# Two raw weights loaded before the attention's last stores, three half tiles made in the attention instead of four, and the sums of later pairs held back

## The chip, the cores and the metric

The kernel runs on one core of a Trainium2 chip. The metric is the device time of one launch in microseconds. Before the change it is 913.08 us, the median of three runs (912.22 to 913.17). The core has five engines with a queue each: PE (TensorE, the matmuls), ACT (ScalarE), DVE (VectorE), POOL (GpSimd) and SP, which here issues every DMA. Each engine takes its queue in order and waits where an operand isn't ready.

## The reference

Attention over 4 batches, 8 heads, 576 positions and 64 elements a head, causal with a window of 128 and a bias linear in the distance; then two feed-forward layers, each 512 -> 2048 -> 512, on 2304 tokens.

```
scores = where(0 <= rel < 128, q @ k.T / 8 - slope[h] * |rel|, -1e9)
x = softmax(scores) @ v                     # to (2304, 512)
h = x @ moe_w_in;   x = (h * cos(h)) @ moe_w_out
h = x @ moe2_w_in;  g = where(h >= 1, h, where(h <= -1, 0, (h + 1)**2 / 4))
out = g @ moe2_w_out                        # (2304, 512)
```

Inputs come as float32 for the attention, while the weights reach the kernel as 64-bit raw words.

## The kernel before, in words

Three of the kernel's habits matter. Every product of the feed-forward layers is made of three passes on TensorE with operands split into a high part (a ScalarE cast) and a low part (a subtraction, line 271). A raw weight of 512 KB is "decoded" to 32 bits by ScalarE and VectorE (lines 700 to 708, `decode`) and then split (lines 759 and 760). And tokens are worked in three chunks of 768: the first chunk of the first layer by plain products (`mm_a`, line 786, then `chain`, lines 795 to 811, then `mm_b`, line 825), the five others by a Strassen-like scheme that needs sums of weight blocks.

A half tile is one raw weight: number j is the input weight (j even) or output weight (j odd) of the column block f = j // 2, 32 in the first layer. The attention (`attention`, line 533) goes over 36 pairs in a pipeline; step k loads the operands of pairs k + 4 and k + 5, computes scores for pair k + 3, and stores x of pair k - 1 where x isn't kept on chip (line 518). SP's list is written in program order, so from step 13 on each step's loads stand behind the store of x of the step before. Beside this the attention "makes" the first half tiles: `halves` (line 325) is a generator that does one instruction group at each `make()`. `D_STEPS` (line 42) says at which steps `make()` is called; two more calls and a loop that empties the generator stand in the attention's tail (lines 609 to 616), ahead of the last copy and store of x. `stage_raw` (line 282) issues the load of a raw tile into one of three buffers, and after it any store of a made tile that is waiting.

After the attention everything of the two layers is put as operations into a planner (`Plan`). It takes TensorE's order as given, works out from costs (`COST`) when each operation is due, and simulates the engines from time 6.0 on; the order in which its simulated engines begin the operations is the order in which they are written to each queue. Where an operation has `after`, the simulation doesn't begin it earlier. None of these times is kept on the chip: there only the order and the data hold.

In the plan, `first_weights` loads, decodes and splits the half tiles that the attention didn't make. For every two column blocks, a pair p, `sum_steps` (line 310) makes the sums: four POOL steps (line 313), then twice a ScalarE cast (line 317), a POOL subtraction (line 271) and a store of 512 KB. For p < `EARLY` they follow at once on the decoded pair. For later pairs the decoded pair is stored to `ud` (line 768) and loaded again (`load_sum`, line 667) into one of two buffers `up`, which the input weights of the last four column blocks use too. The sums are needed by the second chunk (line 876 on). The second layer's weights are loaded from planned time 178 on.

Of the kernel before, what the change touches and what calls it, by code (L numbers as in the profile page):

```python
# [30 lines left out]
UNITS = (("A11", "A12"), ("S3", "S1"), ("S2", "S4"), ("A22",))  # L31


MADE = 4


AHEAD = 3
W2_FROM, W2_STEP = 178.0, 33.0
EARLY = 3


D_STEPS = (4, 9, 11, 13, 14, 15, 16, 18, 20)
PT = "DADADADD"
XE = "DA"
ORDERED = {ENG.DVE, ENG.Activation, ENG.Pool, ENG.SP}
# [187 lines left out]
def attention_moe_moe_kernel(  # L233
# [91 lines left out]
    def halves():  # L325

        def low_part(f, h):
            w = (win, wout)[h][f]
            u = (half_u(win_u[0], f), wout_u.get(f))[h]
            sub_lo(DVE, w[:, 1, :], u, w[:, 0, :])  # L330
            if not h:
                stores.append((lambda: move(fd[0][0][3], w[:, :, 256:512])) if f else (lambda: move(fd[0][0][0], w)))

        before = None
        for j in range(MADE):
            f, h = j // 2, j % 2
            stage_raw(0, j)
            if j + 1 < MADE:
                stage_raw(0, j + 1)
            t = raw64.pop((0, j))  # L340
            low, high = words(t)
            if h:
                wout_u[f] = u = two.tile([128, 512], F32, tag="wu", name=nm("wu"), bufs=U_BUFS)
            else:
                if f == 0:
                    win_u[0] = big("W", NF, "up", F32, (128, 4, 256))
                u = half_u(win_u[0], f)
            ui = u32(u)
            ACT.activation(u, high.bitcast(F32), AF.Copy, scale=2.0**-112)
            yield  # L350
            DVE.tensor_scalar(out=ui, in0=ui, scalar1=3, scalar2=0x7FFFFFFF,
                              op0=ALU.logical_shift_left, op1=ALU.bitwise_and)
            yield
            DVE.scalar_tensor_tensor(out=ui, in0=high, scalar=0x80000000, in1=ui,
                                     op0=ALU.bitwise_and, op1=ALU.bitwise_or)
            yield
            DVE.scalar_tensor_tensor(out=ui, in0=low, scalar=29, in1=ui,
                                     op0=ALU.logical_shift_right, op1=ALU.bitwise_or)
            if h:
                wout[f] = w = big("W", NF, "wo")  # L360
            else:
                win[f] = w = big("Q", Q_BUFS, "wi")
            ACT.copy(w[:, 0, :], u)
            if before:
                yield
                low_part(*before)
            before = f, h
        yield
        low_part(*before)
# [163 lines left out]
    def attention():  # L533
        for part in range(2):
            for n in range(3):
                load(n, (part,))
        make_identity(nc, ident)
        make_dist8()
        DVE.memset(half, 0.5)
        DVE.memset(half_pi, TWO_PI / 4)  # L540
        np_ = len(pairs)
        for k in range(-AHEAD, np_ - AHEAD - 1):
            new = pairs[k + AHEAD]
            mid = pairs[k + AHEAD - 1] if k + AHEAD >= 1 else None
            nrm = pairs[k + AHEAD - 2] if k >= 2 else None
            cur = pairs[k] if k >= 0 else None
            old = pairs[k - 1] if k >= 1 else None
            if k > -AHEAD:
                load(k + AHEAD + 1)
                load(k + AHEAD + 2)  # L550
            if k == 0:
                pe_t(cur)
            pe_s(new)
            if k > 0:
                pe_t(cur)
            if old:
                pe_v(old)
            scores(new, 0)
            if cur:
                copy_t(cur, 0)  # L560
            if nrm:
                normalise(nrm)
            if k >= 1:
                prepare(mid)
            scores(new, 1)

            if k in D_STEPS:
                make()
            while low_parts:
                low_parts.pop()()  # L570
            if mid:
                invert(mid, add=k < 1)
                if k < 1:

                    normalise(mid)
            if cur:
                copy_t(cur, 1)
            if old:
                put_x(old)

        p0, p1, p2, p3, p4 = pairs[np_ - 5:]
        pe_s(p4)
        pe_t(p1)
        pe_v(p0)
        scores(p4, 0)
        copy_t(p1, 0, "D")
        normalise(p2)
        invert(p3, add=True)
        normalise(p3)
        copy_t(p1, 1, "A")  # L590
        scores(p4, 1)
        pe_t(p2)
        pe_v(p1)
        copy_t(p2, 0, "D")

        ACT.activation(half_pi2, half, AF.Sin)
        put_x(p0, "A")
        invert(p4, add=True)
        normalise(p4)
        copy_t(p2, 1, "D")  # L600
        pe_t(p3)
        pe_v(p2)
        put_x(p1, "D")
        copy_t(p3, 0, "D")
        copy_t(p3, 1, "A")
        pe_t(p4)
        pe_v(p3)
        put_x(p2, "A")
        make()
        copy_t(p4, 0, "D")  # L610
        copy_t(p4, 1, "A")
        pe_v(p4)
        put_x(p3, "A")
        make()
        for _ in making:
            pass
        put_x(p4, "A")
        while stores:
            stores.pop(0)()
# [43 lines left out]
            gate = [part(kt, "T4", t4, k + 4)]  # L663
        return bt

    def load_sum(op, p, s, reads):
        op("S", "512", lambda: SP.dma_start(s.t, ud[p]), reads=reads, writes=[s])

    def moes():

# [10 lines left out]
            held.append(b)  # L681
            return b

        for f in range(2):
            wo[0][f] = ready("W", wout[f])
            wi[f] = ready("Q", win[f])
        pair0 = ready("W", win_u[0])
        g_res = [Res() for _ in range(NF)]
        for r in g_res:
            r.t = None  # L690
        kept = {tag: [b for b in held if b.tag == tag] for tag in ("W", "Q")}
        plan = Plan({"s": S_BUFS, "Q": Q_BUFS, "B": 14, "W": NF, "ld": LD_BUFS, "wu": U_BUFS, "so": SO_BUFS, "up": UP_BUFS},
                    {"s": [8.0] * 4, "ld": [9.0], "wu": [8.0], **kept})
        op = plan.op

        def s_buf(name, dtype=F32):
# [46 lines left out]
        def first_weights(j):  # L743
            f, h = j // 2, j % 2
            p = f // 2
            raw = Buf("ld", lambda: two.tile([128, 512], mybir.dt.int64, tag="ld", name=nm("wst"), bufs=LD_BUFS))
            op("S", "512", lambda: SP.dma_start(raw.t, w1[f, h]), writes=[raw])
            if h:
                u = Buf("wu", lambda: two.tile([128, 512], F32, tag="wu", name=nm("wu"), bufs=U_BUFS))
                ap = lambda: u.t  # L750
                wo[0][f] = w = Buf("W", lambda: big("W", NF, "wo"))
            else:
                if f % 2 == 0:
                    wi_u[p] = Buf("W", lambda: big("W", NF, "up", F32, (128, 4, 256))) if f < 12 else Buf("up", pair_tile)
                u = wi_u[p]
                ap = lambda: half_u(u.t, f)
                wi[f] = w = Buf("Q", lambda: big("Q", Q_BUFS, "wi"))
            decode(raw, u, ap)
            op("A", "hi512", lambda: ACT.copy(w.t[:, 0, :], ap()), reads=[u], writes=[w])
            op("D", "tt512", lambda: sub_lo(DVE, w.t[:, 1, :], ap(), w.t[:, 0, :]), reads=[u], writes=[w])  # L760
            if h:
                return
            if f % 2 == 0:
                op("S", "512", lambda: move(fd[0][p][0], w.t), reads=[w], writes=[fac[0][p][0]])
                return
            op("S", "256", lambda: move(fd[0][p][3], w.t[:, :, 256:512]), reads=[w], writes=[fac[0][p][3]])
            if p >= EARLY:
                op("S", "512", lambda: SP.dma_start(ud[p], u.t), reads=[u], writes=[ud_res[p]])
            else:
                sum_steps(op, 0, p, u, lambda: Buf("so", part_tile), lambda i: fac[0][p][i])  # L770
# [170 lines left out]

        sum_steps(op, 0, 0, pair0, lambda: Buf("so", part_tile), lambda i: fac[0][0][i])
        for f in range(NF):
            if 2 * f >= MADE:
                first_weights(2 * f)
                first_weights(2 * f + 1)
            mm_a(0, f)
            chain(0, f)
            if f:
                mm_b(0, f - 1)  # L950
            last = mm_a(1, f)
            chain(1, f)
            for g in (f - 2, f - 1) if f == 2 else (f - 1,) if f > 2 else ():
                mm_b(1, g)
            if f == 4:
                bt = prep(op, 0, 1, "DP", [last])
        for p in range(EARLY, NP):
            s = Buf("up", pair_tile)
            load_sum(op, p, s, [ud_res[p]])
            sum_steps(op, 0, p, s, lambda: Buf("so", part_tile), lambda i, p=p: fac[0][p][i])  # L960
        second_weights()
        fills = carry()
# [149 lines left out]
```

## Time and profile before

| | |
|---|---|
| median of three runs | 913.08 us |
| profiled execution: time, span | 916.26 us, 914.4 us |
| PE busy | 882.4 us (96%) |
| DVE, ACT, POOL busy | 668.9, 552.9, 264.2 us |
| granted PE clock, mean | 0.991 |
| DMA moved | 190.29 MB, 208 GB/s |

All times in the rows are microseconds from the start of the span. The attention's last matmul ends at about 127.5, the first chunk lasts to about 275, and the second chunk begins there. From 282 on PE hardly ever stands still. A row of a timeline may merge several like instructions (x12): its duration then reaches from the first to the last. In brackets stands the idle time of the engine before it and what ended it.

### The profile page before, as it was taken

What the parts mean: (1) busy time and instruction counts of PE and PEld (TensorE: products, weight loads), DVE (VectorE), ACT (ScalarE), POOL (GpSimd) and SP (SyncE); (2) the same over time, 40 slices, a digit from 0 to 9 for tenths busy, and PEclk for the clock granted to TensorE, in tenths of its full rate; (3) what the DMA queues carried; (4) which work ended last, traced back from release to release, by engine and by line L of the source; (5) the groups of instructions that cost most, each with busy time, mean ns of one, the idle gap of its engine ahead of it and who ended that gap; (6) DMA issues with size and microseconds to landing.
All of it is one profiled execution on the core that took longest, in us unless ns stands there. A gap on an engine that the chain in (4) does not pass through costs nothing. (4 is left out here: it accounts for less than half of the span.)

```text
span 914.4 us, 15792 instructions
## 1 busy us (share of the span) xinstructions
PE 882.4 (96%) x5472; PEld 832.2 (91%) x5472; DVE 668.9 (73%) x1404; ACT 552.9 (60%) x1257; POOL 264.2 (29%) x269
## 2 busy tenths in 40 slices
PE   7998987998999999999999999999999999999998
PEld 5776776877889999999999899999999999999998
DVE  6896869999875687997887897877555558355551
ACT  7886857877766577667777565655344445344440
POOL 5665654358332011671211750302200004000000
PEclk9998998999999999999999999999999999999999
DMA  8546736876887678658879578875154452444210
GB/s 300 176 136 209 213 119 207 298 260 229 267 298 249 207 250 311 242 211 318 277 285 328 196 264 312 271 277 182 49 196 161 162 168 75 138 161 162 93 35 34
DMA packets 81262, 190.29 MB, mean 208 GB/s; under 512 B 8224, under 2 KB 40992, under 8 KB 81184
## 3 DMA queue, kind: packets, MB, share of 16 engines
q1 hardware_dynamic: 81184, 189.30, 61.2%
q8 instruction: 43, 0.70, 0.3%
q14 instruction: 35, 0.29, 0.1%
HBM read 140.51 MB, written 48.76 MB: 207 GB/s over the span
## 5 line engine op out<-in xcount | busy, mean ns | idle before, releaser
L937 PE MATMUL y<-gh,wo 128*128 128x384 f32 x1280 | 339.5, 335 | 0.0
L876 PE MATMUL h<-b,wi 128*128 128x384 f32 x1680 | 305.5, 334 | 0.7 <-ACT c L884 0.6
L876 PEld LDWEIGHTS h<-b,wi 128*128 128x128 f32 x1680 | 292.2, 188 | 1.6 <-ACT c L884 0.9
L937 PEld LDWEIGHTS y<-gh,wo 128*128 128x128 f32 x1280 | 233.4, 188 | 0.0
L937 PE MATMUL y<-gl,wo 128*128 128x384 f32 x640 | 215.1, 336 | 2.8 <-DVE gl L271 2.7
L937 PEld LDWEIGHTS y<-gl,wo 128*128 128x128 f32 x640 | 120.7, 189 | 4.9 <-DVE gl L271 4.9
L313 POOL TENSOR_TENSOR up<-up 128x256 f32<-128x256 f32 x64 | 62.2, 972 | 212.2 <-DVE so L271 170.2
L884 ACT COPY c<-h 128x384 f32<-128x384 f32 x120 | 57.3, 478 | 94.5 <-PE h L876 90.4
L888 DVE TENSOR_TENSOR c<-h,c 128x384 f32<-128x384 f32 x120 | 66.4, 553 | 50.0 <-PE h L876 26.3
L914 ACT ACTIVATE t<-t,half 128x384 f32<-128x384 f32 x96 | 59.0, 618 | 59.1 <-DVE t L911 59.1
L451 ACT ACTIVATE sc<-sc,st 128x256 f32<-128x256 f32 (+1 forms) x144 | 70.1, 489 | 25.7 <-DVE st L444 22.3
L271 DVE TENSOR_TENSOR gl<-t,gh 128x384 fp32r<-128x384 f32 (+1 forms) x96 | 59.7, 622 | 33.5 <-ACT gh L894 29.9
L457 POOL TENSOR_TENSOR sc<-sc,st 128x512 f32<-128x512 f32 (+1 forms) x72 | 70.0, 993 | 41.8 <-DVE st L531 30.5
L643 POOL TENSOR_TENSOR xs<-xs,xs 128x384 f32<-128x384 f32 x20 | 26.6, 1331 | 180.4 <-DVE b L271 123.8
L786 PE MATMUL h<-x,wi 128*128 128x512 f32 (+1 forms) x384 | 72.3, 339 | 4.5 <-DVE t L801 4.5
L786 PEld LDWEIGHTS h<-x,wi 128*128 128x128 f32 x384 | 59.9, 190 | 13.8 <-DVE t L801 5.8
L271 DVE TENSOR_TENSOR gl<-g,gh 128x384 fp32r<-128x384 f32 x80 | 59.3, 778 | 7.2 <-PE y L937 3.1
L444 DVE CUSTOM_DVE_ANT_0 sc<-pa,dist 128x256 f32<-128x256 f32 (+1 forms) x144 | 52.4, 402 | 11.6 <-PE pa L429 11.4
L924 DVE TENSOR_TENSOR g<-c,t 128x384 f32<-128x384 f32 x80 | 47.6, 597 | 18.1 <-ACT t L914 9.8
L705 DVE TENSOR_SCALAR wst<-wst 128x512 uint16<-128x512 uint16 x60 | 52.3, 871 | 10.9 <-ACT wst L702 10.4
L271 POOL TENSOR_TENSOR so<-up,so 128x512 fp32r<-128x512 f32 x32 | 46.2, 1455 | 45.0 <-ACT so L317 45.0
L894 ACT CAST gh<-t 128x384 fp32r<-128x384 f32 x80 | 41.1, 514 | 18.1 <-DVE t L917 17.2
(90 smaller groups left out, 1230.3 us busy)
## 6 DMA issues: line engine op xcount, KB each, us to landing
wi<-fd SPq DMA_DIRECT2D x120, 512.0 KB, 4.6
wst<-in_w SPq DMA_DIRECT2D x64, 512.0 KB, 4.7
fd<-so SPq DMA_DIRECT2D x40, 512.0 KB, 4.9
qk<-in_qkv SPq DMA_DIRECT2D x36, 320.0 KB, 3.8
wi<-fd SPq DMA_DIRECT2D x40, 256.0 KB, 3.3
xs<-xd SPq DMA_DIRECT2D x40, 192.0 KB, 4.6
v<-in_qkv SPq DMA_DIRECT2D x36, 192.0 KB, 3.8
out_t<-ys SPq DMA_DIRECT2D x24, 192.0 KB, 1.9
```

Of the source, the lines that this page charges most:

```text
L271: eng.tensor_tensor(out=out, in0=full, in1=f32(hi), op=ALU.subtract)
L313: op("P", "tt256", lambda i=i, x=x, y=y, alu=alu: POOL.tensor_tensor(out=s.t[:, i, :], in0=s.t[:, x, :], in1=s.t[:, y, :], op=alu), writes ...
L444: DVE.tensor_tensor_reduce(out=sc[:, h, 0:w], in0=b[h], in1=dist8[2 * hp + h][:, 256 - w:256], scale=-0.125, scalar=3.0e38, op0=ALU.add, o ...
L451: ACT.activation(sc[:, h, 0:w], sc[:, h, 0:w], AF.Exp, bias=st[:, c:c + 1], scale=-1.0, accum_out=st[:, 4 + c:5 + c])
L457: POOL.tensor_tensor(out=sc[:, :, 0:w], in0=sc[:, :, 0:w], in1=st[:, 8 + 2 * j:10 + 2 * j].unsqueeze(2).to_broadcast([128, 2, w]), op=ALU. ...
L705: op("D", "ts16", lambda: DVE.tensor_single_scalar(out=quarters(raw.t)[:, :, 1], in_=quarters(raw.t)[:, :, 3], scalar=0x8000, op=ALU.bitwi ...
L786: PE.matmul(h, lhsT=wi[f].t[:, k, s], rhs=x, start=(n == 0), stop=(n == 11))
L876: PE.matmul(cell.t, lhsT=unit.t[:, a, s], rhs=bs[kt].t[:, x, :], start=(start and i == 0), stop=(stop and i == 5), skip_group_check=True)
L884: op("A", "copy384", lambda: ACT.copy(s.t, cell.t), reads=[bank[tag]], writes=[s])
L888: op("D", "tt384", lambda: DVE.tensor_tensor(out=s.t, in0=cell.t, in1=s.t, op=ALU.add), reads=[bank[tag]], writes=[s])
L914: op("A", "f384", lambda: ACT.activation(t.t, t.t, AF.Square, bias=half, scale=0.5), writes=[t])
L937: PE.matmul(cell.t, lhsT=w[:, a, s], rhs=x.t, start=(first and i == 0 and k == 0), stop=(last and i == 1 and k == 2), skip_group_check=True)
```

## The change

`MADE` goes from 4 to 3, so the output weight of block 1 (half tile 3) is no longer made in the attention. Instead, when the third half tile is begun, the raw loads of half tiles 3 and 4 are both issued, and the plan finds them as held buffers (`staged`) and only decodes them. `D_STEPS` gets one more step, 3, and the tail has one `make()` in place of the emptying loop. `EARLY` goes from 3 to 2, so that pair 2's sums go through `ud` as well, and `load_sum` gets a time, 64 + 15.6 p, before which the planner doesn't begin it.

```
-MADE = 4
+MADE = 3
-EARLY = 3
+EARLY = 2
+SUM_FROM, SUM_STEP = 64.0, 15.6
-D_STEPS = (4, 9, 11, 13, 14, 15, 16, 18, 20)
+D_STEPS = (3, 4, 9, 11, 13, 14, 15, 16, 18, 20)
...
-            if j + 1 < MADE:
-                stage_raw(0, j + 1)
+            stage_raw(0, j + 1)
+            if j + 1 == MADE:
+                stage_raw(0, j + 2)
...
         put_x(p3, "A")
         make()
-        for _ in making:
-            pass
+        make()
         put_x(p4, "A")
...
+    def load_sum(op, p, s, reads, after):
+        op("S", "512", lambda: SP.dma_start(s.t, ud[p]), reads=reads, writes=[s], after=after)
...
+        staged = {j: ready("ld", t) for (_, j), t in raw64.items()}
...
-                    {"s": [8.0] * 4, "ld": [9.0], "wu": [8.0], **kept})
+                    {"s": [8.0] * 4, "wu": [8.0], **kept})
...
+            raw = staged.get(j)
+            if not raw:
+                raw = Buf("ld", lambda: two.tile([128, 512], mybir.dt.int64, tag="ld", name=nm("wst"), bufs=LD_BUFS))
+                op("S", "512", lambda: SP.dma_start(raw.t, w1[f, h]), writes=[raw])
...
-            load_sum(op, p, s, [ud_res[p]])
+            load_sum(op, p, s, [ud_res[p]], SUM_FROM + SUM_STEP * p)
```

## Rows read from the trace of the kernel before

**Rows 1.** PE's waits from 127 to 282: total us, times, longest.
```profile
PE y L825 <- ACT gh L810: 7.4, 1, 7.4
PE h L786 <- DVE t L801: 4.5, 5, 1.5
PE y L825 <- DVE g L271: 1.9, 2, 1.0
```

**Rows 2.** PE's timeline in the first chunk: start, us, instruction, [idle before].
```profile
127.47 7.20 PE L786 MATMUL h<-x,wi 128*128 128x512 f32 x36
142.09 0.79 PE L825 MATMUL y<-gh,wo 128*128 128x512 f32 x1 [7.43 <-ACT gh L810]
...
158.24 2.91 PE L786 MATMUL h<-x,wi 128*128 128x512 f32 x12
...
166.57 2.91 PE L786 MATMUL h<-x,wi 128*128 128x512 f32 x12
...
193.07 3.02 PE L786 MATMUL h<-x,wi 128*128 128x512 f32 x12 [1.32 <-DVE t L801]
...
241.55 3.06 PE L786 MATMUL h<-x,wi 128*128 128x512 f32 x12 [0.49 <-DVE t L801]
```

**Rows 3.** Busy time by engine from 142 to 147, granted clock, DMA.
```profile
142.00:147.00 5.00, 4.91 (x12) 3.65 (x13) 4.88 (x7) 4.12 (x10) 1.40 (x1) 0.58 0.46 184
```

**Rows 4.** ACT's timeline around the long wait.
```profile
130.69 0.36 ACT L514 COPY x<-pa 128x256 f32<-128x256 f32 x1
136.17 0.66 ACT L700 ACTIVATE up<-wst 128x512 f32<-128x512 f32 x1 [5.12 <-DMA wst<-in_w]
...
137.28 0.58 ACT L795 ACTIVATE k<-h 128x512 int32<-128x512 f32 x1
...
141.42 0.62 ACT L810 CAST gh<-t 128x512 fp32r<-128x512 f32 x1
```

**Rows 5.** DVE's timeline: the attention's tail, the first decode, a later low part.
```profile
128.25 0.43 DVE L351 TENSOR_SCALAR wu<-wu 128x512 uint32<-128x512 uint32 x1 [1.12 <-ACT wu L349]
...
130.81 0.69 DVE L271 TENSOR_TENSOR wo<-wu,wo 128x512 fp32r<-128x512 f32 x1
137.41 0.74 DVE L705 TENSOR_SCALAR wst<-wst 128x512 uint16<-128x512 uint16 x1 [5.90 <-ACT wst L702]
...
156.28 0.73 DVE L271 TENSOR_TENSOR wi<-up,wi 128x512 fp32r<-128x512 f32 x1
```

**Rows 6.** SP's timeline: DMA issues in the attention, at its end, and later.
```profile
68.95 0.43 SPq L286 DMA_DIRECT2D wst<-in_w  x1
...
72.46 0.47 SPq L415 DMA_DIRECT2D qk<-in_qkv  x1
...
115.50 15.90 SPq L518 DMA_DIRECT2D xd<-x  x7
...
132.16 7.10 SPq L747 DMA_DIRECT2D wst<-in_w  x4
...
246.74 1.76 SPq L667 DMA_DIRECT2D up<-ud  x1
```

**Rows 7.** PE's timeline in the attention, scores of three pairs.
```profile
79.47 2.08 PE L429 MATMUL pa<-qk 64*128 64x256 f32 x8 [3.46 <-DMA qk<-in_qkv]
...
85.07 1.14 PE L429 MATMUL pa<-qk 64*128 64x256 f32 x8
...
88.18 1.22 PE L429 MATMUL pa<-qk 64*128 64x256 f32 x8
```

**Rows 8.** Groups from 127 to 282: count, busy us, mean ns, idle before.
```profile
L313 POOL TENSOR_TENSOR up<-up 128x256 f32<-128x256 f32 x32 | 30.6, 957 | 40.2 <-DMA up<-ud 24.2 <-DVE wi L271 7.7 <-ACT wo L363 6.5
L271 POOL TENSOR_TENSOR so<-up,so 128x512 fp32r<-128x512 f32 x16 | 23.4, 1476 | 28.6 <-ACT so L317 28.6
L708 DVE SCALAR_TENSOR_TENSOR up<-up,wst 128x512 uint32<-128x512 uint32 x14 | 13.4, 957 | 0.1
L801 DVE TENSOR_TENSOR t<-h,t 128x512 f32<-128x512 f32 x16 | 11.0, 688 | 1.4 <-ACT t L800 1.4
```

More of the change, by code (lines that the diff above doesn't have):

```diff
@@ L664, in prep @@
         return bt
-    def load_sum(op, p, s, reads):
-        op("S", "512", lambda: SP.dma_start(s.t, ud[p]), reads=reads, writes=[s])
+    def load_sum(op, p, s, reads, after):
+        op("S", "512", lambda: SP.dma_start(s.t, ud[p]), reads=reads, writes=[s], after=after)
     def moes():
@@ L682, in ready @@
             return b
-        for f in range(2):
-            wo[0][f] = ready("W", wout[f])
-            wi[f] = ready("Q", win[f])
+        for f, t in wout.items():
+            wo[0][f] = ready("W", t)
+        for f, t in win.items():
+            wi[f] = ready("Q", t)
+        staged = {j: ready("ld", t) for (_, j), t in raw64.items()}
         pair0 = ready("W", win_u[0])
@@ L690, in moes @@
             r.t = None
-        kept = {tag: [b for b in held if b.tag == tag] for tag in ("W", "Q")}
+        kept = {tag: [b for b in held if b.tag == tag] for tag in ("W", "Q", "ld")}
         plan = Plan({"s": S_BUFS, "Q": Q_BUFS, "B": 14, "W": NF, "ld": LD_BUFS, "wu": U_BUFS, "so": SO_BUFS, "up": UP_BUFS},
-                    {"s": [8.0] * 4, "ld": [9.0], "wu": [8.0], **kept})
+                    {"s": [8.0] * 4, "wu": [8.0], **kept})
         op = plan.op
@@ L745, in first_weights @@
             p = f // 2
-            raw = Buf("ld", lambda: two.tile([128, 512], mybir.dt.int64, tag="ld", name=nm("wst"), bufs=LD_BUFS))
-            op("S", "512", lambda: SP.dma_start(raw.t, w1[f, h]), writes=[raw])
+            raw = staged.get(j)
+            if not raw:
+                raw = Buf("ld", lambda: two.tile([128, 512], mybir.dt.int64, tag="ld", name=nm("wst"), bufs=LD_BUFS))
+                op("S", "512", lambda: SP.dma_start(raw.t, w1[f, h]), writes=[raw])
             if h:
@@ L943, in moes @@
         for f in range(NF):
-            if 2 * f >= MADE:
-                first_weights(2 * f)
-                first_weights(2 * f + 1)
+            for j in (2 * f, 2 * f + 1):
+                if j >= MADE:
+                    first_weights(j)
             mm_a(0, f)
```

## The prediction

> **What bounds the kernel now.** I read three views in order: who the engines waited for, TensorE's timeline around its longest wait, and then the other queues over the same microseconds. TensorE is busy for 96% of the span, so a change pays only where TensorE stands still or runs at the lower clock. Between the attention and the second chunk it waits for three things: once, 7.4 us, for a ScalarE cast of gh; five times, 4.5 us in all, for VectorE's product h*t; and twice, 1.9 us, for VectorE's low part of g [rows 1]. Together that is 13.8 us.
>
> The long wait lies at the start of the first product. TensorE begins it at 127.47, issues 36 matmuls in 7.20 us and then stands from 134.67 to 142.09 [rows 2]. The reader should follow that cast backwards. It belongs to a chain of ScalarE and VectorE that starts with a ScalarE step k at 137.28; ScalarE did nothing from about 131.05 to 136.17 because the instruction ahead of k, the decode of a raw weight, waited 5.12 us for its DMA [rows 4]. VectorE was idle 5.90 us for the same reason [rows 5]. That DMA was issued only at 132.16: SP takes its list in order, and its last seven stores of x hold it from 115.50 to 131.40 [rows 6]. The last store needs a ScalarE copy at 130.69, which stands behind the making of the fourth half tile [rows 4]. So one late store delays a load, the load blocks ScalarE's queue, and the blocked queue delays TensorE.
>
> **The change, part by part.** *Raw weights.* Half tiles 3 and 4 are now in the buffer long before the end of attention. ScalarE is free after the last copy of x. Without the fourth half tile ahead of it that copy waits for TensorE alone, which ends the attention at 127.47 [rows 2], so it ends near 127.9. Four decode steps of some 0.55 us (136.17 to 137.28 holds two [rows 4]) end at 130.1. The first product's h is ready after 12 of the 36 matmuls; 12 such matmuls take 2.91 us [rows 2], hence 130.4. So k can start at 130.4. Before, from the start of k at 137.28 to TensorE's restart at 142.09 were 4.8 us with decode steps between them [rows 2, 4]; I keep that length and get 135.2, where TensorE is ready at 134.67. The hole shrinks from 7.43 to about 0.5: -6.9. At best it goes fully, -7.4. At worst the load that is still late (the third raw buffer, issued near 128.5 behind the last x store) stands before k in ScalarE's order; with the 4.0 us from issue to decode [rows 4, 6] k would start at 133.1 and TensorE at 137.9, a hole of 3.2, or -4.2. I expect the better case, since that tile shares its 32-bit buffer with half tile 4 and can't be decoded before it.
>
> *Clock.* After the hole the granted clock is 0.58 for 5 us, and 12 matmuls take 4.91 us there [rows 3] against 2.91 us at full speed [rows 2]: 2.0 us at the lower level, 1.2 GHz. With a hole of 0.5 I count it all as gain, -2.0. After the waits of 1.32 and 0.49 us the next 12 matmuls took 3.02 and 3.06 us [rows 2], nearly the full clock. The other end is 0.
>
> *The fourth half tile.* From the attention's tail go three VectorE steps and a low part, the first of them after a wait of 1.12 us; VectorE ends there at 131.5 [rows 5] and should end near 127. The planned part gets a decode instead: three ScalarE steps, and on VectorE two decode steps and a low part of some 0.7 us each (the step at 137.41 and the low part at 130.81 [rows 5]), 2.1 us. These fall into the 5.90 us that VectorE lost before; if that cover is gone they delay the chains by 2.1 us at most. The tile is needed for the second output product, which comes after some 7 us more of TensorE work. I count 0. The made tiles' steps shift by one place in the attention; TensorE hardly waits there outside the one place below.
>
> *Sums held back.* A pair's sums are four POOL steps of 957 ns and two of 1476 ns, 6.8 us; 32 of the first kind, so all eight lots, run between 127 and 282 [rows 8]. While POOL works VectorE's steps are stretched: the decode's last step averages 957 ns there, against 688 ns of h*t, which has the same shape [rows 8]. The seven waits of 6.4 us lie between 193 and 242 [rows 2]. Spread evenly, one lot per 19 us, the 80 us from 163 to 243 hold four lots. After the change pair p is held to 64 + 15.6p on the planner's clock. Its 6.0 is TensorE's 127.47, so pairs 2 and 3 start near 217 and 232 and the other four after 247: two lots remain in these 80 us, half. I take half of 6.4 us, rounded up because VectorE also starts sooner: -3.5. Bounds: all, -6.4; none, 0, if TensorE, now 9 us earlier, asks VectorE for the same work sooner. Pair 2 adds a store and a load of 512 KB; SP's queue has room for them and I count 0.
>
> Weighed against this: the Trainium skill ("SBUF — State Buffer", section "Who interferes with whom") says that a VectorE step with two SBUF inputs and a GpSimd step reading SBUF exclude each other for a whole instruction, while a step with at most one SBUF input doesn't contend. The trace agrees in kind: h*t, with h in PSUM, averages 688 ns and is not stretched [rows 8]. By the rule a lot could cost VectorE up to 6.8 us, two lots more than the 6.4 us of stalls, and the sum would end at 899.5 instead of 902.4.
>
> *The burst in the attention.* This speaks against the change. At 68.95 a raw load, with the made tile's store right behind it, pushed the qk load of 72.46 [rows 6] back until TensorE stood 3.46 us; it then ran 8 matmuls in 2.08 us instead of 1.14, and that step took 5.60 us (79.47 to 85.07) against 3.11 for the next [rows 7]. So the burst, two transfers of 512 KB, cost 3.46 + 2.5 = 6.0 us. Now three such transfers stand in one step, two steps earlier. Half as many bytes again: half of 3.46 more, +1.7; the slow stretch after it stays as long. Bounds: -6.0, if the new place misses the loads' narrow lead, and +5, if two loads come late.
>
> The sum: -6.9 - 2.0 - 3.5 + 1.7 = -10.7 us. The rest of the kernel is TensorE-bound and I leave it as it is, within 1 us. The profiled execution's span is 914.4 us, inside 916.26 us; the span lies 1.3 us above the median of the runs, 913.08. So 914.4 - 10.7 - 1.3 = 902.4.
>
> **The rivals.**
> 1. *The hole only narrows.* In-order ScalarE meets another late load before k. For it: the planner believed the loads much earlier than they came, and it still does for half tiles 5 and 6. Against it: two raw tiles are there, which fills ScalarE until k. Hole 3.2 (-4.2), clock half kept (-1.0), stalls -2.0, burst +1.7: -5.5, 907.6.
> 2. *VectorE gives it back.* It, not TensorE, sets the pace from 150 to 242, and the stalls stay at 6.4 or grow by up to 2. For it: the waits of rows 1 are all for VectorE. Against it: a weight's low part is done at 157.0 and used at 166.57, 9.6 us ahead [rows 2, 5]. -6.9 - 2.0 + 1.0 + 1.7 = -6.2, 906.9.
> 3. *Slower: a held sum blocks SP.* The load for a sum waits in SP's list for one of two buffers, which the sums and the last four input half tiles share, and the raw loads queue behind it. Before, such a load held SP 1.76 us at most [rows 6]. It decides once it holds SP longer than the 9.6 us by which weights are ahead. Were each of the six to hold it 12 us, TensorE would lose 6 x 2.4 = 14.4 us, against 10.7 gained: 916.8.
> 4. *The burst is harmless.* Six microseconds gained instead of 1.7 lost: -7.7 more, 894.7.
>
> **How the numbers follow.** The forecast has 0.60 (own range 898 to 906), rivals 1 and 2 have 0.11 each, rival 4 has 0.06, rival 3 has 0.06, and 0.06 is left for gains and losses that cancel near 913. Faster by over 0.2% (1.8 us, about what a measurement of this kernel can tell from no change) takes the forecast and rivals 1, 2 and 4: 0.88; same 0.06; slower 0.06. The range from 894.5 to 909.5 holds these four and leaves out the last two and the tails.
>
> **What would show it.** In the new trace: the raw decode on ScalarE starts near 128 without a DMA wait, k of the first product near 130.4, and TensorE's wait before the first output product is under 1.5 us at full clock. VectorE's h*t waits sum to 2 to 4 us instead of 6.4. TensorE's wait for qk in the attention moves some two steps earlier and lasts about 5 us. POOL's sums of pair 2 come near 210 or later, and the second chunk starts about 11 us sooner. The prediction is wrong if the hole stays above 3 us, if the first 12 matmuls after it run at half clock, if the waits of rows 1 on VectorE stay as they are, or if new TensorE waits name the factors' loads.

## The result and the profile after

The changed kernel takes 902.27 us, the median of four runs (902.0 to 904.03), against 913.12 us (912.22 to 916.73) for the kernel before on the same chip: ratio 0.9878, 95% interval 0.9849 to 0.9907. The forecast was 902.4. The profiled execution took 902.43 us with a span of 900.7, that of before 916.26 with 914.4.

I cut each span in three, since each part of the change acts in one: the attention, up to the first matmul of the first chunk; the chunk, up to the second chunk's first matmul; and the rest.

| | attention | chunk | rest | span |
|---|---|---|---|---|
| before | 127.5 | 147.6 | 639.4 | 914.4 |
| changed | 127.4 | 132.9 | 640.4 | 900.7 |

So the whole gain, 14.7 us, comes from the first chunk, and about 1 us is lost behind it. Here is TensorE's timeline of the changed kernel, the rows that answer to [rows 2] (line numbers have moved by 2 to 5):

```profile
127.38 7.24 PE L791 MATMUL h<-x,wi 128*128 128x512 f32 x36
...
135.19 0.50 PE L830 MATMUL y<-gh,wo 128*128 128x512 f32 x1 [0.58 <-ACT gh L815]
...
136.07 0.50 PE L830 MATMUL y<-gl,wo 128*128 128x512 f32 x1 [0.38 <-DVE gl L272]
...
184.11 3.01 PE L791 MATMUL h<-x,wi 128*128 128x512 f32 x12 [0.70 <-DVE t L806]
...
204.33 0.50 PE L830 MATMUL y<-gl,wo 128*128 128x512 f32 x1 [0.31 <-DVE gl L272]
...
260.23 1.21 PE L881 MATMUL h<-b,wi 128*128 128x384 f32 x6
```

The hole of 7.43 us is now 0.58 and 0.38, and of the seven later waits on VectorE only short ones are left, 0.70 and 0.31. ScalarE shows why the hole is gone, beside [rows 4]:

```profile
127.49 0.37 ACT L516 COPY x<-pa 128x256 f32<-128x256 f32 x1 [0.45 <-PE pa L496]
127.76 0.66 ACT L703 ACTIVATE up<-wst 128x512 f32<-128x512 f32 x1
128.33 0.65 ACT L703 ACTIVATE wu<-wst 128x512 f32<-128x512 f32 x1
128.89 1.22 ACT L705 ACTIVATE wst<-wst 128x512 int32<-128x512 uint16 x2
130.53 0.60 ACT L800 ACTIVATE k<-h 128x512 int32<-128x512 f32 x1 [0.42 <-PE h L791]
...
134.52 0.61 ACT L815 CAST gh<-t 128x512 fp32r<-128x512 f32 x1
```

After the last copy of x it goes straight into the decode, no row waits for a DMA, and k waits for its product only. Behind the hole the clock is full, where [rows 3] had 0.58 (busy time by engine, then granted clock, DMA share, GB/s):

```profile
135.00:139.00 4.00, 3.43 (x15) 2.69 (x16) 4.00 (x7) 3.83 (x9) 1.44 (x1) 1.00 0.89 330
```

SP in step 16 issues three transfers of 512 KB within 1.5 us, and TensorE's scores pay for it; the second fence answers to [rows 7]:

```profile
63.18 0.42 SPq L287 DMA_DIRECT2D wst<-in_w  x1
63.81 0.33 SPq L279 DMA_DIRECT2D fd<-wi  x1
64.18 0.42 SPq L287 DMA_DIRECT2D wst<-in_w  x1
...
65.55 0.91 SPq L417 DMA_DIRECT2D qk<-in_qkv  x1
...
128.97 0.59 SPq L752 DMA_DIRECT2D wst<-in_w  x1
```

```profile
66.06 1.13 PE L431 MATMUL pa<-qk 64*128 64x256 f32 x8
74.27 2.08 PE L431 MATMUL pa<-qk 64*128 64x256 f32 x8 [5.47 <-DMA qk<-in_qkv]
78.64 1.13 PE L431 MATMUL pa<-qk 64*128 64x256 f32 x8
```

The load of 65.55 is used at 74.27: 5.47 us of waiting instead of 3.46, and half the clock again for those eight matmuls.

### The profile page after: what moved, and what is told of

It is laid out like the page before. It is cut to its first block, busy times and chain, and to the rows that moved or that the text cites. A ratio compares the mean times of both kernels' runs of the same rounds, so it can differ in the third digit from the quotient of the medians.

```text
span 900.7 us, 15815 instructions
## 1 busy us (share of the span) xinstructions
PE 878.1 (97%) x5472; PEld 828.1 (92%) x5472; DVE 660.0 (73%) x1403; ACT 553.6 (61%) x1258; POOL 258.1 (29%) x269
## 4 chain that ended last, share of the span: by engine, by line
PE 84%; DVE 5%; POOL 4%; issue 3%; DMA 2%; ACT 2%; SPq 0%; POOLq 0%; ACTq 0%; DVEq 0%
PE h L881 31%; PE y L942 31%; PE y L830 6%; PE h L791 5%; PE pa L431 4%; PE pa L471 4%; PE pa L496 4%; POOL up L314 1%; DMA qk<-in_qkv 1%; DVE wst L708 1%; POOL b L272 1%; DVE gl L272 1%; DVE b L272 1%; POOL T L644 1%; DVE up L711 1%
## 5 line engine op out<-in xcount | busy, mean ns | idle before, releaser
L942 PEld LDWEIGHTS y<-gl,wo 128*128 128x128 f32 x640 | 120.1, 188 | 5.3 <-DVE gl L272 5.2
L889 ACT COPY c<-h 128x384 f32<-128x384 f32 x120 | 57.5, 479 | 87.7 <-PE h L881 83.0
L314 POOL TENSOR_TENSOR up<-up 128x256 f32<-128x256 f32 x64 | 59.0, 922 | 174.4 <-DVE so L272 122.8
L893 DVE TENSOR_TENSOR c<-h,c 128x384 f32<-128x384 f32 x120 | 66.4, 553 | 47.1 <-PE h L881 24.7
L453 ACT ACTIVATE sc<-sc,st 128x256 f32<-128x256 f32 (+1 forms) x144 | 70.2, 489 | 25.4 <-DVE st L446 23.7
L929 DVE TENSOR_TENSOR g<-c,t 128x384 f32<-128x384 f32 x80 | 49.7, 621 | 19.1 <-ACT t L919 10.3
L708 DVE TENSOR_SCALAR wst<-wst 128x512 uint16<-128x512 uint16 x61 | 50.0, 826 | 7.3 <-ACT wst L705 7.0
L431 PE MATMUL pa<-qk 64*128 64x256 f32 (+1 forms) x288 | 44.1, 425 | 9.3 <-DMA qk<-in_qkv 9.3
```

The costliest lines, as they stand in the source:

```text
L314: op("P", "tt256", lambda i=i, x=x, y=y, alu=alu: POOL.tensor_tensor(out=s.t[:, i, :], in0=s.t[:, x, :], in1=s.t[:, y, :], op=alu), writes ...
L431: PE.matmul(b[h], lhsT=t[r, j * 128:j * 128 + 128], rhs=t[r, kc:kc + w], start=True, stop=True)
L453: ACT.activation(sc[:, h, 0:w], sc[:, h, 0:w], AF.Exp, bias=st[:, c:c + 1], scale=-1.0, accum_out=st[:, 4 + c:5 + c])
L708: op("D", "ts16", lambda: DVE.tensor_single_scalar(out=quarters(raw.t)[:, :, 1], in_=quarters(raw.t)[:, :, 3], scalar=0x8000, op=ALU.bitwi ...
L889: op("A", "copy384", lambda: ACT.copy(s.t, cell.t), reads=[bank[tag]], writes=[s])
L893: op("D", "tt384", lambda: DVE.tensor_tensor(out=s.t, in0=cell.t, in1=s.t, op=ALU.add), reads=[bank[tag]], writes=[s])
```

## The experiments

Each kernel was profiled and timed beside the kernel before. The table has all of them; the sections read them. "Waits" are TensorE's waits for VectorE in the chunk behind the hole; in the first profile of before they sum to 6.5 us.

| kernel | attention | hole | waits | chunk | rest | median us | ratio (95%) |
|---|---|---|---|---|---|---|---|
| before, again | 122.8 | 7.9 | 5.3 | 148.9 | 639.5 | 913.62 | 1.0007 (0.9991 to 1.0023) |
| e1 raw part only | 127.1 | 1.0 | 4.3 | 138.5 | 639.7 | 906.72 | 0.9922 (0.9903 to 0.9940) |
| e2 held sums only | 125.7 | 7.8 | 1.6 | 141.8 | 639.3 | 907.27 | 0.9928 (0.9909 to 0.9948) |
| e4 burst spread | 120.1 | 1.0 | 0.9 | 132.8 | 640.4 | 895.47 | 0.9803 (0.9783 to 0.9822) |
| e5 no early loads | 119.7 | 5.5 | 1.2 | 141.0 | 640.3 | 903.12 | 0.9880 (0.9850 to 0.9911) |
| e6 four made, one ahead | 123.1 | 6.9 | 6.3 | 147.7 | 638.1 | 912.70 | 0.9998 (0.9980 to 1.0016) |
| e7 not held | 125.3 | 1.0 | 4.8 | 139.2 | 640.2 | 905.47 | 0.9906 (0.9879 to 0.9933) |
| e8 pair 2 at once | 126.2 | 1.0 | 1.4 | 133.4 | 639.5 | 900.77 | 0.9859 (0.9835 to 0.9883) |
| e9 spread, pair 2 at once | 120.7 | 1.0 | 1.4 | 133.4 | 639.7 | 895.77 | 0.9792 (0.9773 to 0.9811) |
| e10 before, burst spread | 121.8 | 7.4 | 5.1 | 148.5 | 639.5 | 910.51 | 0.9959 (0.9938 to 0.9980) |
| e11 store moved | 126.3 | 1.0 | 1.0 | 132.9 | 640.4 | 901.08 | 0.9849 (0.9828 to 0.9869) |

### The two parts, each alone (e1, e2)

```
e1, on the changed kernel:  EARLY = 3;  SUM_FROM, SUM_STEP = 0.0, 0.0
e2, on the kernel before:   EARLY = 2;  load_sum(..., after=64.0 + 15.6 * p)
```

> The change without its second part: half tiles 3 and 4 loaded ahead and three made, but pair 2 summed at once again and no sum held back. Theory A (the terms add up): the hole ahead of the first output product is about 1.0 us as in the changed kernel, the half clock is gone, and the VectorE waits stay near the 6.4 us of before; the second chunk starts near 266.7 and the time is 913.1 - 6.5 - 1.9 = 904.7. Theory B (VectorE sets the pace until about 242): TensorE, which comes sooner, waits longer for VectorE, 10 us or more instead of 6.4; the second chunk starts near 270.5 and the time is about 908.5.

> The kernel before with only the sums held back (pair 2 through memory, the times 64 + 15.6 p). Theory A: the hole of 7.4 us and the half clock stay, the VectorE waits fall from 6.4 to under 1.5 us, the second chunk starts near 269.5 and the time is 913.1 - 5.5 = 907.6. Theory C (with the hole open TensorE is late anyway, so the sums matter only once it is closed): the waits hardly move or the gain is under 2 us, 911 to 914.

TensorE's waits in e1 behind the hole, and in e2 at the hole and behind it:

```profile
184.07 3.01 PE L791 MATMUL h<-x,wi 128*128 128x512 f32 x12 [0.78 <-DVE t L806]
192.01 1.58 PE L830 MATMUL y<-g,wo 128*128 128x256 f32 x11 [0.40 <-DVE g L272]
202.88 3.02 PE L791 MATMUL h<-x,wi 128*128 128x512 f32 x12 [0.89 <-DVE t L806]
206.85 0.50 PE L830 MATMUL y<-gl,wo 128*128 128x512 f32 x1 [0.73 <-DVE gl L272]
214.44 3.06 PE L791 MATMUL h<-x,wi 128*128 128x512 f32 x12 [1.53 <-DVE t L806]
```

```profile
140.68 0.80 PE L826 MATMUL y<-gh,wo 128*128 128x512 f32 x1 [7.76 <-ACT gh L811]
202.10 0.50 PE L826 MATMUL y<-gl,wo 128*128 128x512 f32 x1 [0.65 <-DVE gl L272]
205.15 1.70 PE L787 MATMUL h<-x,wi 128*128 128x256 f32 x12 [0.21 <-DVE t L802]
207.73 1.57 PE L826 MATMUL y<-g,wo 128*128 128x256 f32 x11 [0.77 <-DVE g L272]
```

Against the chunk of 148.2 (mean of the two profiles of before) the raw part shortens it by 9.8 us and the held sums by 6.5; both together by 15.4, so the terms add up to within 1 us, as theory A has it. B, in which TensorE waits more for VectorE the sooner it comes, fell: the waits are 4.3, not 10. C, in which the sums matter only once the hole is closed, fell too. e1's second chunk starts where A put it (265.55 for 266.7), but its time is 2.0 us above A's 904.7: A took its gain off the median of before and left out that e1 has the changed kernel's burst, three transfers in one step.

### The kernel before once more (e3), and the burst spread (e4)

```
             yield
+            if j == 1:
+                stage_raw(0, 3)          # step 13
...
             yield
+            while j == 2 and stores:     # step 20, no longer in stage_raw
+                stores.pop(0)()
```

> The kernel before, unchanged, for a second profile: its profiled execution was 3.1 us above its median. If the burst in the attention varies from one execution to the next, the TensorE wait for qk near 76 (3.46 us) and the slow step behind it differ by about that much and the second chunk starts near 272; if the executions differ elsewhere, both stay and the difference lies after 275.

> The changed kernel with its burst in the attention spread: the raw load of half tile 3 issued in step 13, that of half tile 4 in step 16, and the made tile's store in step 20, instead of all three in step 16. Theory A (the burst makes the qk loads late): the TensorE wait for qk of 5.5 us falls under 1 us, the clock stays at 1.00 there, the last matmul of the attention ends near 121.5 instead of 127.4, and the time is 902.3 - 6 = 896.3. Theory D (the loads are late by themselves, since each stands behind a store of x): the wait stays at 3 us or more and the time falls by less than 2 us, to 900.5 or above.

The scores that wait, in e3 and then in e4:

```profile
76.75 1.14 PE L429 MATMUL pa<-qk 64*128 64x256 f32 x8 [1.97 <-DMA qk<-in_qkv]
```

```profile
68.62 1.14 PE L433 MATMUL pa<-qk 64*128 64x256 f32 x8 [0.76 <-DVE up L353]
```

The same code waited 1.97 us here and 3.46 in the first profile [rows 7], and only in the first did the clock drop behind it. The attention ended 4.7 us apart: 1.2 us of that lie ahead of the wait, 1.5 in it and 2.0 behind it. So the burst's price varies from one execution to the next. In e4 no score waits for a load any more, the attention ends at 120.1 and the kernel takes 895.47 us, 0.8 us under what theory A said. D, in which the loads are late by themselves, fell. This version beats both kernels.

### What closes the hole (e5, e6)

```
e5, on the changed kernel:        if j + 1 < MADE:
                                      stage_raw(0, j + 1)
e6, on the kernel before:   -     if j + 1 < MADE:
                            +     (always)
                                      stage_raw(0, j + 1)     and `staged` as in the change
```

> The changed kernel (three made, sums held) without the early loads: half tiles 3 and 4 are loaded by the plan, behind the last store of x. Compared by the length of the first chunk, from its first matmul to the second chunk's first (before 147.6 and 148.9, changed 132.9), since the attention's burst changes too. Theory L (the late load blocks ScalarE): the load is issued near 1.6 us after the chunk's start instead of 4.7, and as before it takes 9.9 us from there to the first output product, so the hole is about 4.3 us and the chunk 136.5 to 138. Theory M (what held the chain was the fourth half tile's making, not the load): hole about 1 us, chunk 133.

> The kernel before (four made, sums as before) with half tile 4 loaded ahead, when the fourth is begun. Theory L: ScalarE is free after its last copy, 3.6 us after the chunk's start, decodes two steps of 0.55 and begins the chain near 4.7, so the hole is 4.7 + 4.8 - 7.2 = 2.3 us; the half clock goes, the VectorE waits stay near 6: chunk 148.2 - 5.3 - 2 = 141. Theory M: the making itself still delays it, hole 5 us or more, chunk 145 or longer.

ScalarE ahead of k, and TensorE behind the hole, first in e5, then in e6:

```profile
126.48 0.66 ACT L702 ACTIVATE up<-wst 128x512 f32<-128x512 f32 x1 [6.26 <-DMA wst<-in_w]
127.05 0.64 ACT L704 ACTIVATE wst<-wst 128x512 int32<-128x512 uint16 x1
127.77 0.68 ACT L702 ACTIVATE wu<-wst 128x512 f32<-128x512 f32 x1
128.34 0.58 ACT L799 ACTIVATE k<-h 128x512 int32<-128x512 f32 x1
132.44 0.79 PE L829 MATMUL y<-gh,wo 128*128 128x512 f32 x1 [5.52 <-ACT gh L814]
```

```profile
126.64 0.69 ACT L700 ACTIVATE up<-wst 128x512 f32<-128x512 f32 x1
127.23 0.66 ACT L702 ACTIVATE wst<-wst 128x512 int32<-128x512 uint16 x1
133.01 0.66 ACT L700 ACTIVATE wu<-wst 128x512 f32<-128x512 f32 x1 [5.12 <-DMA wst<-in_w]
133.57 0.58 ACT L797 ACTIVATE k<-h 128x512 int32<-128x512 f32 x1
137.26 0.80 PE L827 MATMUL y<-gh,wo 128*128 128x512 f32 x1 [6.93 <-ACT gh L812]
```

Both show the late load as what blocks ScalarE, and both cost more than theory L said. In e5 (three made, nothing loaded ahead) the hole is 5.5 us, where 4.3 was expected; the half clock follows it (0.50 from 132 to 138). In e6 the first decode runs at once, but the planner now puts the decode of the next raw weight ahead of k as well, and that load came at 133.01: the hole is 6.9, not 2.3, and the kernel gains nothing. That is rival 1's mechanism, in a kernel with one raw tile ahead instead of two. By its numbers alone e6 would fit theory M, in which the making itself holds the chain (hole 5 us or more, chunk 145 or longer). M is wrong all the same: e5 makes three and still has the hole, and in e6 ScalarE is done with the fourth making at 126.4 and idles for 5.12 us behind the first decode, for a DMA.

The other side of e5: its attention ends at 119.7. In the changed kernel the early loads give 8.1 us in the chunk (141.0 to 132.9) and cost 6.6 us in the attention (119.7 to 127.4, of which 1.1 us are there by the scores at 57 us, ahead of the burst). By the medians the two kernels are equal, 0.9878 and 0.9880.

### Which half of the sums' part counts (e7, e8)

```
e7, on the changed kernel:  SUM_FROM, SUM_STEP = 0.0, 0.0     (EARLY = 2)
e8, on the changed kernel:  EARLY = 3                         (64.0 + 15.6 * p)
```

> The changed kernel with pair 2 summed from memory (EARLY 2) but no time before which a sum may begin. Theory H (the holding back is what counts): POOL works as much between 193 and 242 as in the kernel with the raw part only (26.3 us), VectorE waits stay near 4 us and the chunk is 137 to 139 us. Theory P (that pair 2 leaves the early stretch is enough): chunk 133 to 134.5.

> The changed kernel with pair 2 summed at once again (EARLY 3), pairs 3 to 7 held to 64 + 15.6 p. Theory H: the waits lay behind 190, where pair 2's sums no longer run, so the chunk is as short as in the changed kernel or 1 us longer: 132.9 to 134. Theory P: 136 to 138.5, since the VectorE time that pair 2's sums take near 155 is missing later.

Busy time of PE, PEld, DVE, ACT and POOL between 193 and 242, in the kernel before, the changed one, e1, e7 and e8:

```profile
193.00:242.00 49.00, 43.75 (x242) 37.51 (x243) 47.75 (x67) 37.41 (x74) 28.50 (x24) 1.00 0.78 265
```

```profile
193.00:242.00 49.00, 48.65 (x275) 42.34 (x274) 45.47 (x75) 39.94 (x78) 20.02 (x18) 1.00 0.74 247
```

```profile
193.00:242.00 49.00, 45.67 (x253) 38.95 (x253) 46.44 (x66) 38.03 (x77) 26.28 (x22) 1.00 0.80 267
```

```profile
193.00:242.00 49.00, 45.68 (x248) 37.95 (x247) 45.84 (x64) 36.73 (x73) 27.62 (x23) 1.00 0.79 263
```

```profile
193.00:242.00 49.00, 48.40 (x276) 42.25 (x276) 44.89 (x76) 40.29 (x79) 12.25 (x11) 1.00 0.70 236
```

Theory H holds: with POOL at 26 to 28.5 us TensorE gets 44 to 46 us of the 49, with POOL at 12 to 20 us it gets 48.5; e2, whose hole is still open, lies between (POOL 16.5, TensorE 47.4). e7's chunk, 139.2, is just above H's range and far from P's, e8's is in H's. Sending pair 2 through memory (e7 against e1) does nothing alone. Without it, e8 and e9 have a chunk 0.5 and 0.7 us longer and no worse a time: `EARLY = 2` is not needed.

### The burst by itself (e9, e10, e11)

```
e9, on e4:                  EARLY = 3
e10, on the kernel before:  raw load of half tile 3 in step 14, store in the tail
e11, on the changed kernel: the store alone moved to step 20
```

> The spread burst of e4 with pair 2 summed at once (EARLY 3), all later sums held. e8 was 1.5 us below the changed kernel, of which 1.15 us was an attention that ended sooner. If that was the burst's variation: chunk 132.8 to 133.5, attention's last matmul near 120.1, time within 0.7 us of e4's 895.5. If pair 2's way through memory itself costs (a store and a load of 512 KB, and sums later in the second chunk): 893.5 to 894.5.

> The kernel before with only its burst spread: the raw load of half tile 3 in step 14, the made tile's store in the tail. Its attention ended at 127.5, 122.8, 125.7 and 123.1 in the profiles of four kernels that share it (mean 124.8), and at 120.1 without a burst. Theory A (burst, and nothing else, is what these lose): it ends near 120, the hole of 7.4 to 7.9 stays, chunk 147.5 to 149, time 913.4 - 4.7 = 908.7. Theory F (the gain of e4 came from elsewhere, its earlier raw load or store): attention at 123 or later, 911 or above.

> The changed kernel with only the store moved from step 16 to step 20, so that step 16 has the two raw loads. Theory N (what counts is how many transfers of 512 KB come together): two cost about what the two of the kernel before cost, the attention ends near 124 and the time is 902.3 - 2.5 = 900. Theory W (the write to memory is what holds up the loads): wait for qk under 1 us, attention near 120.5, time 896.

The scores that wait in e11; in e10 no score waits for a load:

```profile
72.11 2.08 PE L431 MATMUL pa<-qk 64*128 64x256 f32 x8 [3.46 <-DMA qk<-in_qkv]
```

e10 gains 0.41% over the kernel before (0.9959), 3.7 us where theory A said 4.7, and its hole is as before. Its attention ends at 121.8, between A's 120 and F's 123, because it reached the burst late: from the scores at 58.24 us on it takes 63.6 us, e4's from the same pair on 63.8. So the burst alone explains what e4 gains, as A has it. e9 equals e4 (895.77). In e11 the wait falls to 3.46 us, as N said; the attention ends at 126.3, not near 124, and the time, 901.08, is 1.1 us above N's 900. W, in which the write holds up the loads, fell. Against the kernel before, e11's 0.9849 and the changed kernel's 0.9878 have intervals that overlap, and from the same pair's scores on its attention takes 69.2 us, that of the changed kernel 70.2. Moving the store alone gained little or nothing: the two raw loads carry most of the price, and how much is the store's stays open.

## Why the prediction was right

**The hole, -6.9 and -2.0.** Right by its own steps: k was forecast for 130.4 and TensorE's restart for 135.2; they came at 130.53 and 135.19. The two waits there sum to 0.96 us, so 6.5 us went, with the full clock behind it. e5 and e6 show the cause, a load that stands before k in ScalarE's order.

**The fourth half tile, 0.** Nothing in the chunk waits for it; e1 differs from the kernel before in the raw part only and has no wait that names its tile.

**The held sums, -3.5.** This term was mis-sized. It argued that half of POOL's work in the stretch goes and with it half of the 6.4 us. POOL's work between 193 and 242 fell by 30% (28.5 to 20.0 us), or by 38% if one takes the same stage of the changed kernel, 9 us earlier (17.7 us between 184 and 233); yet the waits fell by 5.5 us, from 6.5 to 1.0. In the chunk the part is worth 6.5 us alone (e2) and 5.6 on top of the raw part (e1 to changed). TensorE waits for what VectorE lacks in the stretch, not for a share of POOL's work: VectorE was busy for 47.75 of 49 us and is for 45.47, and a little room was enough. By the rule of the Trainium skill that it weighed ("SBUF — State Buffer", "Who interferes with whom") the prediction had -6.4 for this term, nearer than its own -3.5.

How POOL takes VectorE's time can be read step by step in the first profile of before:

```profile
202.01 0.67 DVE L708 SCALAR_TENSOR_TENSOR wu<-wu,wst 128x512 uint32<-128x512 uint32 x1
...
220.47 3.48 POOL L313 TENSOR_TENSOR up<-up 128x256 f32<-128x256 f32 x3
222.05 0.70 DVE L801 TENSOR_TENSOR t<-h,t 128x512 f32<-128x512 f32 x1
...
226.73 3.01 POOL L271 TENSOR_TENSOR so<-up,so 128x512 fp32r<-128x512 f32 x2 [2.78 <-ACT so L317]
226.86 1.71 DVE L708 SCALAR_TENSOR_TENSOR up<-up,wst 128x512 uint32<-128x512 uint32 x1
```

The decode's last step, with both operands in SBUF, takes 0.68 us on average over its 16 instances in the chunk with no POOL step beside them, and 1.3 us over the 10 that have one beside them for more than half their time. h*t, with one operand in SBUF, takes 0.68 and 0.70. The prediction had it that one operand in SBUF spares a step; not every such step is spared: the decode's first VectorE step (L705) has one, and takes 0.75 and 1.13. Over all its decode and low-part steps of 512 columns VectorE lost about 7.6 us in the 49 us from 193 to 242 of before, and in the same stage 4.3 in the changed kernel, 10.0 in e1, 11.1 in e7 and 2.5 in e8 (my estimate: their durations less what they take without POOL). That is the room that holding back gives. Averaged over the whole chunk it hardly shows: the decode's last step has 898 and 909 ns for its two destinations, where before it had 957 and 868, since the held sums still run, only later.

```profile
L711 DVE SCALAR_TENSOR_TENSOR wu<-wu,wst 128x512 uint32<-128x512 uint32 x15 | 13.6, 909 | 0.0
L711 DVE SCALAR_TENSOR_TENSOR up<-up,wst 128x512 uint32<-128x512 uint32 x14 | 12.6, 898 | 0.1
L806 DVE TENSOR_TENSOR t<-h,t 128x512 f32<-128x512 f32 x16 | 11.0, 687 | 2.4 <-ACT t L805 2.4
```

**The burst, +1.7.** The wait grew by 2.0 us (3.46 to 5.47), at step 16 instead of 18, as said. The executions begin up to 2 us apart, so I count the attention from the start of one pair's scores ahead of the burst, here in before and in the changed kernel, to the chunk's first matmul:

```profile
58.22 0.92 PE L429 MATMUL pa<-qk 64*128 64x256 f32 x8
```

```profile
57.21 0.92 PE L431 MATMUL pa<-qk 64*128 64x256 f32 x8
```

It takes 69.3 us in that profile of before and 70.2 in the changed kernel; on average 67.0 in the four profiles with the burst of before, 69.4 in the four with three transfers, and 63.6 to 64.0 in the four where the burst is spread or absent. So three transfers cost about 5.7 us and two 3.2, a difference of 2.4 where 1.7 was put; the profile that I reckoned from was an execution with a dear burst (5.5, close to the 6.0 of the prediction). The shifted steps, put at 0, gave back 1 us: two waits of TensorE for ScalarE of 0.5 us, at 26.7 and 56.6 in before, are gone. Against the medians the attention lost more: a run of before at the median has a span near 911.3, so by its chunk and rest its attention ended near 123.7 (an estimate), and the changed kernel pays 3.7 us.

**The rest, 0.** It is 640.4 us against 639.4: two waits of 0.50 and 1.05 us at 393 and 402, which name steps c (L889, L893). Waits there, 0.7 to 1.6 us in all, come in every kernel that makes three half tiles and in none that makes four. Why is open.

So the sum of -10.7 and the measured -10.85 agree partly because errors cancel: the chunk gained about 3 us more than the 12.4 that the prediction summed for it, some 2 of it in the sums, and the attention and the rest cost about 3 us more. That is luck. Two of the signs named in advance did not come as said: the h*t waits sum to 0.70 us and not 2 to 4, and the second chunk starts 14.8 us sooner, not 11. Rivals 1 to 3 did not come: the late load was issued at 128.97 but stood behind k, no load for a sum held SP longer than 0.5 us, and no wait in the chunk names a DMA. Rival 4 had the right place but not the right kernel: the harmless burst is e4, and it is worth the 6.8 us that separate the two.

## What to carry to other kernels

A queue that is taken in order turns one late load into a stop of everything behind it, so look at what the planner put ahead of the urgent step and load that early; one tile early is useless if the next one stands there too. Here ScalarE's 5.12 us made 7.43 us of TensorE's. An early load has to be put where the DMA queue has room: three transfers put in one step gave back most of what the early loads had won (6.6 of 8.1 us in the profiles, and by the medians all of it), and spreading them over steps 13, 16 and 20 brought another 0.75%. And take the reference for a sum from an execution near the median, since a wait that varies moves the whole ledger.

## What was not expected of the hardware

The clock behind a wait of like length was not the same in two executions of the same code. In the chunk, at the same place, TensorE waited 1.54 us in the first profile of before and 1.53 us in e3:

```profile
222.81 3.01 PE L786 MATMUL h<-x,wi 128*128 128x512 f32 x12 [1.54 <-DVE t L801]
```

```profile
219.46 4.41 PE L786 MATMUL h<-x,wi 128*128 128x512 f32 x12 [1.53 <-DVE t L801]
```

Behind the first the granted clock was 1.00 (222.8 to 227), behind the second 0.66 (219.4 to 223.9), and the same 12 matmuls took 1.4 us more. In the attention of the same two executions the clock fell behind a wait of 3.46 us (0.52 from 79 to 85, eight matmuls in 2.08 us) and stayed at 1.00 behind one of 1.97 us; 2.0 of the 4.7 us by which the attentions end apart lie behind those waits.
